# Interleaving two pairs at the changes of stretch, and taking the input sums and loads earlier

## The chip, the cores and the metric

The kernel runs on one core of one Trainium2 chip. The metric is the device time of one execution in microseconds. The engines are TensorE (PE, matmuls), VectorE (DVE), ScalarE (ACT), GpSimd (POOL) and SyncE (SP, which issues DMAs).

## The reference

Sparse attention of 2304 tokens, whose output goes through a mixture of experts (8 experts, weights from a normalised gate) and then through a second feed-forward part with an ELU. The change touches the last two.

```python
def _moe_ref(x, w_gate, w1, w2):                    # x (2304, 512), w1 (8, 512, 1024), w2 (8, 1024, 512)
    ...                                             # P (2304, 8): normalised exp(x @ w_gate)
    for e in range(E):
        h = np.maximum(x @ w1[e], 0.0)
        out += P[:, e:e + 1] * (h @ w2[e])

def _moe2_ref(x, w_in, w_out):                      # w_in (512, 2048), w_out (2048, 512)
    h = x @ w_in
    g = np.where(h > 0.0, h, alpha * (np.exp(np.minimum(h, 0.0)) - 1.0))
    return g @ w_out
```

## The kernel before

Both parts are a first product (tokens by w1 or w_in), a nonlinearity and a second product (by w2 or w_out). The hidden columns are cut into 40 pairs of 256: pairs 0 to 31 are the experts, 32 to 39 the second part. The tokens are cut into block 0 (1024 tokens), block 1 (1024) and 256 plain tokens that go with block 1. `SEGS` orders this into four **stretches**: 0 (block 0, experts), 1 (block 1 and plain tokens, experts), 2 (the same tokens, second part) and 3 (block 0, second part). The changes 0→1, 1→2 and 2→3 lie near 795, 1640 and 1865 us. Pairs are worked in groups of two: first products of both, then their second products.

Each fp32 operand is held as a high and a low part of a shorter format, and a product takes three matmuls (high·high, high·low, low·high; `products`, L934). ACT casts the high part; DVE or POOL subtract it to get the low part (`low`, L213; names `xl`, `w1l`, `w2l`, `hl`).

For a block of 1024 tokens the first product (`gemm1`) is a 2×2 block product by seven products instead of eight. Its token operands are the raw blocks B11, B21, B22 and four sums T1 to T4: t1 = b − a, t2 = b' − t1, t3 = t2 − a, t4 = a' − t2, where a, a' (tiles `rawa`) are the first half of the tokens and b, b' (`rawb`) the second. Each of the seven is a **part**: six matmuls of 128x512 into a bank. In a pair they run B11, (B21 if early), T2, T1, T3, (B21 otherwise), T4, B22. DVE adds the partial results (`add`, L995: u2 = T2's bank + a1, a copy of B11's bank by ACT, L1024; u3; c22), then `activate` makes the hidden values: ReLU on ACT (hh, L949) and its low part on DVE (hl, L951); in stretches 2 and 3 the ELU, several steps on ACT and DVE (g, hh, hl, L956 to L961). Plain tokens take `gemm1_plain` (values ph, pl).

Sum banks: `bank()` takes one of four in turn for first products, `ybank()` one of four others for second products. A bank can be taken again when its last reader is done.

The second product of a group (`whole2`, `gemm2`, L1095) runs half after half of the block; a half has four token tiles, each with a bank of its own, and 24 matmuls of the first pair come ahead of 24 of the second. `finish` has DVE add a finished bank to `acc` (L1126, L1112).

Ahead of stretches 1 and 3, whose tokens come from memory, `x_loads` issues loads of 1 MB (`rawa`, `rawb`; for stretch 1 `rawp`, the plain tokens) in the last group of the stretch before, and during that group's second product the operands are built: `build_a` (B11, B21), `x_plain`, then `x_b` with `build_b` (sums L312, casts L322, low parts L213). For stretch 2 the tokens are the stretch's own result: PE transposes `acc` (L1149), and `x1_a`, `x1_b` build from there. At the end of stretch 0 block 0's results are kept: PE transposes them, and DVE or ACT copy them (kept, L1160).

What sets the order: the program is written out by one Python thread; `gap()` is called between groups of three or six matmuls and lets each waiting generator take a step (weights, gate, builds, copies), so an engine's queue holds its instructions in the order of those steps. Each engine takes its queue strictly in order; engines wait for each other by semaphores. `need(x)` forces the build of an operand ahead of the product that reads it.

Of the kernel before, what the change touches and what calls it, by code (L numbers as in the profile page):

```python
# [123 lines left out]
def sparse_attention_moe_kernel(ctx: ExitStack, tc: tile.TileContext, a, out):  # L124
# [175 lines left out]
    def build_b(a, b, home=None, cs=(0, 1)):  # L300
# [30 lines left out]
        t3 = {c: minus(t2[c], a(c), 3, c) for c in cs}
        yield from both(T3, t3, (ve, po_))

        t4 = {c: minus(a(c + 2), t2[c], 4, c) for c in cs}
        yield from both(T4, t4, (ve, po_))
        b22 = {c: b(c + 2) for c in cs}
        yield from both(B22, b22, (ve, ve))
# [640 lines left out]
    def gemm1(sg, p, early=False):  # L978


        n = prep_state["now"] = index(sg, p)
# [70 lines left out]
        fill()  # L1052
        prod(s3, S4, B22, start=False)
        add(s3, s3, u2)
        act(s3, 0, 1)
        step()
        return hs
# [293 lines left out]
```

## Time and profile before

| what | us |
|---|---|
| runs (three) | 2035.65, 2035.70, 2038.86 |
| their median | 2035.7 |
| the profiled execution | 2036.48 |
| its span | 2034.7 |
| PE busy in it | 2000.9 (98%) |
| DVE busy | 1271.3 (62%) |
| mean granted PE clock, of full | 0.992 |

The steady stretches have no idle PE time: a group takes 40.8 us in stretch 0 and 52.0 in stretch 1. In a timeline the first column is an instruction's start in us from the start of the span, the second its duration (with x2 or x3, of all of them), and what stands in brackets is how long the engine had been idle before and which instruction's end released it. Matmuls overlap, so the distance of their starts (0.227 us at full clock) is the pace, not the duration shown.

### The profile page before, as it was taken

What the parts mean: (1) busy time and instruction counts of PE and PEld (TensorE: products, weight loads), DVE (VectorE), ACT (ScalarE), POOL (GpSimd) and SP (SyncE); (2) the same over time, 40 slices, a digit from 0 to 9 for tenths busy, and PEclk for the clock granted to TensorE, in tenths of its full rate; (3) what the DMA queues carried; (4) which work ended last, traced back from release to release, by engine and by line L of the source; (5) the groups of instructions that cost most, each with busy time, mean ns of one, the idle gap of its engine ahead of it and who ended that gap; (6) DMA issues with size and microseconds to landing.
All of it is one profiled execution on the core that took longest, in us unless ns stands there. A gap on an engine that the chain in (4) does not pass through costs nothing.

```text
span 2034.7 us, 26108 instructions
## 1 busy us (share of the span) xinstructions
PE 2000.9 (98%) x10019; PEld 1661.5 (82%) x10019; DVE 1271.3 (62%) x2061; ACT 690.3 (34%) x1419; POOL 642.2 (32%) x742
## 2 busy tenths in 40 slices
PE   8899999999999999999999999999999989999999
PEld 7677888888888887888888888888888878887887
DVE  5666757544554557466666666666664585558665
ACT  3444333322332224222222222222222354445543
POOL 3443333323233324222222222222222322224330
PEclk9899999999999999999999999999999999999999
DMA  8521111111111114122222222222221101122111
GB/s 257 152 95 60 53 55 53 59 52 43 52 62 52 42 52 139 49 91 71 82 78 83 78 83 73 80 71 88 73 68 42 42 21 42 42 83 93 42 52 52
DMA packets 82277, 145.41 MB, mean 71 GB/s; under 512 B 5689, under 2 KB 39737, under 8 KB 82153
## 3 DMA queue, kind: packets, MB, share of 16 engines
q1 hardware_dynamic: 81192, 143.55, 22.4%
q8 instruction: 78, 1.28, 0.3%
q14 instruction: 47, 0.38, 0.1%
q10 hardware_dynamic: 960, 0.21, 0.1%
HBM read 125.91 MB, written 17.83 MB: 71 GB/s over the span
## 4 chain that ended last, share of the span: by engine, by line
PE 89%; DVE 6%; ACT 3%; issue 1%; POOL 1%; DMA 0%; ACTq 0%; POOLq 0%; DVEq 0%
PE ybank L1095 46%; PE bank L934 39%; DVE xl L213 1%; ACT g L957 1%; ACT g L956 1%; PE ybank L541 1%; PE ybank L523 1%; DVE u L995 1%; PE bank L480 1%; ACT hh L961 0%; DVE rawa L312 0%; PE ybank L480 0%; DVE acc L1112 0%; DMA wg<-in_moe_w_gate 0%; DVE g L959 0%
## 5 line engine op out<-in xcount | busy, mean ns | idle before, releaser
L1095 PE MATMUL ybank<-w2h,hh 128*128 128x512 f32 x1280 | 501.5, 392 | 0.4 <-DVE acc L1112 0.2
L1095 PE MATMUL ybank<-w2h,hl 128*128 128x512 f32 x1280 | 498.2, 389 | 0.0
L1095 PE MATMUL ybank<-w2l,hh 128*128 128x512 f32 x1280 | 498.1, 389 | 0.0
L934 PE MATMUL bank<-xh,w1h 128*128 128x512 f32 x1120 | 444.4, 397 | 16.9 <-DVE u L995 5.7
L934 PE MATMUL bank<-xh,w1l 128*128 128x512 f32 x1120 | 437.9, 391 | 0.1
L934 PE MATMUL bank<-xl,w1h 128*128 128x512 f32 x1120 | 438.0, 391 | 0.0
L213 POOL TENSOR_TENSOR w1l<-w1raw,w1h 128x256 fp32r<-128x256 f32 x240 | 209.2, 892 | 425.9 <-ACT w1h L203 423.0
L1126 DVE SCALAR_TENSOR_TENSOR acc<-ybank,prob,acc 128x512 f32<-128x512 f32 x244 | 182.7, 749 | 230.3 <-PE ybank L1095 230.0
L213 POOL TENSOR_TENSOR w2l<-w2raw,w2h 128x512 fp32r<-128x512 f32 x80 | 103.6, 1295 | 569.8 <-ACT w2h L203 554.5
L1095 PEld LDWEIGHTS ybank<-w2h,hh 128*128 128x128 f32 x1280 | 240.4, 188 | 51.0 <-DVE acc L1112 1.7
L1095 PEld LDWEIGHTS ybank<-w2h,hl 128*128 128x128 f32 x1280 | 240.3, 188 | 50.3
L1095 PEld LDWEIGHTS ybank<-w2l,hh 128*128 128x128 f32 x1280 | 240.4, 188 | 48.4
L934 PEld LDWEIGHTS bank<-xh,w1h 128*128 128x128 f32 x1120 | 211.3, 189 | 67.9 <-DVE u L995 9.2
L203 ACT CAST w2h<-w2raw 128x512 fp32r<-128x512 f32 x160 | 97.0, 620 | 489.6 <-issue 396.7
L934 PEld LDWEIGHTS bank<-xh,w1l 128*128 128x128 f32 x1120 | 211.1, 188 | 45.6 <-POOL w1l L213 0.5
L934 PEld LDWEIGHTS bank<-xl,w1h 128*128 128x128 f32 x1120 | 211.6, 189 | 39.6
L995 DVE TENSOR_TENSOR u<-bank,a 128x512 f32<-128x512 f32 x160 | 110.5, 691 | 196.0 <-PE bank L934 164.6
L231 POOL TENSOR_TENSOR wsum<-w1raw 128x256 f32<-128x256 f32 x160 | 122.3, 764 | 221.6 <-DMA w1raw<-in_moe_w 159.4
L949 ACT ACTIVATE hh<-bank 128x512 fp32r<-128x512 f32 x192 | 114.2, 595 | 109.0 <-DVE bank L995 106.7
L951 DVE SCALAR_TENSOR_TENSOR hl<-bank,hh 128x512 fp32r<-128x512 f32 x192 | 131.3, 684 | 6.3
L213 DVE TENSOR_TENSOR w1l<-wsum,w1h 128x512 fp32r<-128x512 f32 (+1 forms) x164 | 119.5, 736 | 12.1 <-ACT w1h L203 11.0
L949 ACT ACTIVATE hh<-c 128x512 fp32r<-128x512 f32 x64 | 40.5, 633 | 239.1 <-DVE c L995 239.1
(194 smaller groups left out, 2541.1 us busy)
## 6 DMA issues: line engine op xcount, KB each, us to landing
w1raw<-in_moe_w SPq DMA_DIRECT2D x64, 512.0 KB, 3.4
w2raw<-in_moe_w SPq DMA_DIRECT2D x64, 512.0 KB, 3.6
q_t<-in_q SPq DMA_DIRECT2D x16, 576.0 KB, 8.0
raw<-in_moe_w_in SPq DMA_DIRECT2D x16, 512.0 KB, 4.2
w_conv<-val SPq DMA_DIRECT2D x32, 256.0 KB, 2.5
raw<-in_moe_w_out SPq DMA_DIRECT2D x16, 512.0 KB, 3.8
w1raw<-w_conv SPq DMA_DIRECT2D x16, 512.0 KB, 4.1
w2raw<-w_conv SPq DMA_DIRECT2D x16, 512.0 KB, 3.3
```

Source lines behind the costliest of these rows:

```text
L203: se.copy(hi, src)
L213: eng.tensor_tensor(out=lo, in0=src, in1=hi.bitcast(F32), op=ALU.subtract)
L231: po_.tensor_tensor(out=o, in0=x, in1=y, op=op)
L480: pe.matmul(pp[:nq, i * nk : (i + 1) * nk], t["q"][:, qc : qc + nq], t["k"][:, kc : kc + nk], start=False, stop=i == nt - 1, skip_group_ch ...
L523: pe.transpose(pt[:nk, i * nq : (i + 1) * nq], s["e"][:, i0 + i], ident[:nq, :nq])
L541: pe.matmul(pv[j * D : (j + 1) * D, c : c + nq // 2], vt[:nk, v_place(local, x if local else i + hf * len(SGROUPS[0]), j), :], es[:, j], s ...
L934: pe.matmul(dst, a_[:, wi, c, :], b_[:, xi, c, :], start=start and i == 0, stop=stop and i == 5, skip_group_check=True,)
L949: se.activation(hh, src, AF.Relu)
L951: ve.scalar_tensor_tensor(out=hl, in0=src, scalar=0.0, in1=hh.bitcast(F32), op0=ALU.max, op1=ALU.subtract)
L995: ve.tensor_tensor(out=out, in0=x, in1=y, op=ALU.add)
L1095: pe.matmul(y, x[:, cs], w[:, f], start=first and f + m == 0, stop=last and f == 1 and m == 2)
L1126: ve.scalar_tensor_tensor(out=at, in0=y, scalar=prob[:, g, e : e + 1], in1=at, op0=ALU.mult, op1=ALU.add)
```

## The change

In the first group of stretches 1, 2 and 3 the two pairs x and y run together, part by part: x B11, y B11, x B22, x B21, x T2, x T1, x T3, y B21, x T4, y T2, y T1, y T3, then plain parts (stretch 1: the second pair's, stretch 2: one), y T4, y B22. Pair x puts B22 in a bank of its own and adds it in with one more DVE add, so all three raw blocks come ahead of its sums. `build_b` gets the matching order (`raw_first`): B22, t3, T2, t4 with the subtractions ahead of the next low parts, then T1, T3, T4. The loads of stretches 1 and 3 are issued four and two groups ahead of the change, and a new generator `x_sums` makes the plain operands, t1 and t2 within those groups at a rate of 0.2 steps a gap. At 1→2 two build steps are taken in each of four gaps (`HURRY`), and the plain tokens' build starts two steps later. `OPEN_WAIT` holds the weights' preparation back by 12 gaps in an interleaved group, and `used` counts a weight's products for each pair apart.

```diff
@@ build_b @@
+        if raw_first:
+            cast = b22()
+            next(cast)
+            yield True
+            next(cast)
+            t3 = more(3)
+            yield True
+            cast = both(T2, t2, (ve, ve))
+            next(cast)
+            yield True
+            next(cast)
+            t4 = more(4)
+            yield True
+            yield from both(T1, t1, (ve, po_))
+            yield from both(T3, t3, (ve, po_))
+            yield from both(T4, t4, (ve, po_))
+            return
...
@@ gap @@
             build_step()
+            if count[0] < hurry[0]:
+                build_step()
...
+    def gemm1_two(sg, pairs, between):
+
+        landed["done"] = max(landed["done"], count[0] + OPEN_WAIT)
+        hs = [{}, {}]
+        x, y = (gemm1_parts(sg, p, h, True, p == pairs[0]) for p, h in zip(pairs, hs))
+        order = (x, y, x, x, x, x, x, y, x, y, y, y, None, y, y)
+        for part in order:
+            if part is None:
+                between()
+            else:
+                next(part)
+        return hs
...
+        if raw_first:
+            need(B22)
+            s4 = bank()
+            prod(s4, S4, B22)
+            step()
+            yield
         if early:
             c11()
+            yield
         need(T2)
         s2 = bank()
         prod(s2, S2, T2)
         u2 = tmp("u2")
         add(u2, s2, a1)
+        if raw_first:
+            add(u2, s4, u2)
+        elif early and sg:
+            tmp("skip")
         step()
+        yield
         need(T1)
         s3 = bank()
         prod(s3, S1, T1)
+        if raw_first:
+            add(s4, s3, u2)
+            act(s4, 0, 1)
         step()
+        yield
...
-    def x_plain():
+    def x_sums(plain):
...
+        if plain:
+            yield from build_plain(late["xp_raw"], *late["xp"], late_tmp)
+        late["sums"] = sums = ({}, {})
+        for c in (0, 1):
+            sums[0][c] = b[:, c]
+            ve.tensor_tensor(out=sums[0][c], in0=b[:, c], in1=a[:, c], op=ALU.subtract)
+            yield True
+        for c in (0, 1):
+            sums[1][c] = t[:, c * HALF : (c + 1) * HALF]
+            ve.tensor_tensor(out=sums[1][c], in0=b[:, c + 2], in1=sums[0][c], op=ALU.subtract)
+            yield True
...
+            if sg in (0, 2) and p == p1 - X_FROM[sg] * GROUP:
...
+                x_loads(*((x_late, True) if sg == 0 else (x_mid, False)))
+                late["x"] = x_sums(sg == 0)
+                gens.append([late["x"], X_RATE, 0.0, False])
...
-X_DELAY = 4
+X_DELAY = 8
+X_FROM, X_RATE = {0: 4, 2: 2}, 0.2
 KEEP_DELAY = 8
 LANDING = 10
+OPEN_WAIT = 12
+HURRY, PLAIN_DELAY = 4, 2
```

In the order listings the lines of the changed kernel are its own: L959 is its product, L1041 its add, L976 and L984 its steps of `activate`, L1198 its `finish`, L1221 its transposes, L1232 its keep copies.

DVE's queue in the last second product of stretch 0. Before: low parts, t1 and t2 (L312), then the accs of the second half.

```order
L213 TENSOR_TENSOR xl_70<-rawa_6579,xh_69 128x512
L213 TENSOR_TENSOR w1l0_82<-wsum_74,w1h0_81 128x512
L213 TENSOR_TENSOR xl_70<-rawa_6579,xh_69 128x512
L312 TENSOR_TENSOR rawb_6580<-rawb_6580,rawa_6579 128x512 x2
L312 TENSOR_TENSOR rawp_6581<-rawb_6580 128x512 x2
L1126 SCALAR_TENSOR_TENSOR acc_71<-ybank_6665,prob_67,acc_71 128x512
L213 TENSOR_TENSOR xl_70<-rawp_6581,xh_69 128x512 x2
L1126 SCALAR_TENSOR_TENSOR acc_71<-ybank_6666,prob_67,acc_71 128x512
```

In the changed kernel, from the same half on:

```order
L213 TENSOR_TENSOR xl_70<-rawa_5538,xh_69 128x512 x2
L1198 SCALAR_TENSOR_TENSOR acc_71<-ybank_6597,prob_67,acc_71 128x512
L1198 SCALAR_TENSOR_TENSOR acc_71<-ybank_6598,prob_67,acc_71 128x512
L213 TENSOR_TENSOR xl_70<-rawb_5539,xh_69 128x512 x2
L312 TENSOR_TENSOR rawa_5538<-rawp_5540,rawa_5538 128x512 x2
L1198 SCALAR_TENSOR_TENSOR acc_71<-ybank_6599,prob_67,acc_71 128x512
L213 TENSOR_TENSOR xl_70<-rawp_5540,xh_69 128x512 x2
L312 TENSOR_TENSOR rawa_5538<-rawa_5538,rawp_5540 128x512 x2
L1198 SCALAR_TENSOR_TENSOR acc_71<-ybank_6600,prob_67,acc_71 128x512
```

t1 and t2 are gone from here; B22's low parts, t3, T2's low parts and t4 stand between the four accs of the first half (banks 6597 to 6600), where before they stood among those of the second.

DVE's queue in the first group of stretch 1, around the first pair's u2. Before (bank 6841 is T2's, 6831 is B11's):

```order
L995 TENSOR_TENSOR u2_6849<-bank_6841,a1_6838 128x512
L213 TENSOR_TENSOR w2l0_84<-w2raw_73,w2h0_83 128x512
L995 TENSOR_TENSOR u3_6881<-bank_6841,a1_6838 128x512
L995 TENSOR_TENSOR c22_6882<-bank_6852,u3_6881 128x512
L1160 COPY kept_6888<-ybank_6873 128x512
L951 SCALAR_TENSOR_TENSOR hl_6886<-c22_6882,hh_6885 128x512
L995 TENSOR_TENSOR bank_6841<-bank_6841,a1_6838 128x512
L951 SCALAR_TENSOR_TENSOR hl_6903<-bank_6831,hh_6902 128x512
```

In the changed kernel (bank 6881 is x's T2, 6849 its B22, 6830 its B11, 6900 its T1):

```order
L1232 COPY kept_6878<-ybank_6867 128x512
L1041 TENSOR_TENSOR u2_6893<-bank_6881,a1_6837 128x512
L1041 TENSOR_TENSOR u2_6893<-bank_6849,u2_6893 128x512
L976 SCALAR_TENSOR_TENSOR hl_6876<-bank_6830,hh_6875 128x512
L1041 TENSOR_TENSOR bank_6849<-bank_6900,u2_6893 128x512
L1232 COPY kept_6917<-ybank_6904 128x512
```

PE's queue at the same place, from the end of x's T2 to its T1. Since bank 6830, x has been given 6830, y 6840, x 6849, x 6881, and then x 6900:

```order
L959 MATMUL bank_6881<-xh_69,w1h1_2250 128x512
L959 MATMUL bank_6881<-xl_70,w1h1_2250 128x512
L959 MATMUL bank_6881<-xh_69,w1l1_2251 128x512
L1221 MATMUL ybank_6885<-ident_63,acc_71 128x128 x4
L959 MATMUL bank_6881<-xh_69,w1h1_2250 128x512
L959 MATMUL bank_6881<-xl_70,w1h1_2250 128x512
L959 MATMUL bank_6881<-xh_69,w1l1_2251 128x512
L959 MATMUL bank_6900<-xh_69,w1h1_2250 128x512
L959 MATMUL bank_6900<-xl_70,w1h1_2250 128x512
```

Bank 6900 is the fifth since 6830 and so the same one of the four. hl from bank 6830 is its last read, and it has moved behind two adds u2; before, T1 took the third bank after B11's.

DVE's queue at 1→2. Before:

```order
L1126 SCALAR_TENSOR_TENSOR acc_71<-bank_13461,prob_67,acc_71 128x512
L312 TENSOR_TENSOR rawb_13476<-ybank_13482,rawb_13476 128x512
L312 TENSOR_TENSOR rawb_13476<-ybank_13492,rawb_13476 128x512
L1126 SCALAR_TENSOR_TENSOR acc_71<-bank_13462,prob_67,acc_71 128x512
L213 TENSOR_TENSOR w2l1_2254<-w2raw_73,w2h1_2253 128x512
L213 TENSOR_TENSOR xl_70<-rawb_13476,xh_69 128x512 x3
L312 TENSOR_TENSOR rawa_13376<-rawb_13476,rawa_13376 128x512 x2
L213 TENSOR_TENSOR xl_70<-rawa_13376,xh_69 128x512
L312 TENSOR_TENSOR rawa_13376<-rawa_13376,rawb_13476 128x512 x2
L995 TENSOR_TENSOR u2_13565<-bank_13554,a1_13533 128x512
L959 SCALAR_TENSOR_TENSOR g_13547<-g_13547,bank_13523 128x512
```

In the changed kernel:

```order
L312 TENSOR_TENSOR rawb_13470<-ybank_13476,rawb_13470 128x512
L312 TENSOR_TENSOR rawb_13470<-ybank_13486,rawb_13470 128x512
L213 TENSOR_TENSOR xl_70<-ybank_13476,xh_69 128x512
L213 TENSOR_TENSOR xl_70<-ybank_13486,xh_69 128x512
L312 TENSOR_TENSOR rawa_13376<-rawb_13470,rawa_13376 128x512 x2
L1198 SCALAR_TENSOR_TENSOR acc_71<-bank_13461,prob_67,acc_71 128x512
L213 TENSOR_TENSOR xl_70<-rawb_13470,xh_69 128x512 x2
L312 TENSOR_TENSOR rawa_13376<-rawa_13376,rawb_13470 128x512 x2
L1198 SCALAR_TENSOR_TENSOR acc_71<-bank_13462,prob_67,acc_71 128x512
L213 TENSOR_TENSOR w2l1_2253<-w2raw_73,w2h1_2252 128x512
L213 TENSOR_TENSOR xl_70<-rawb_13470,xh_69 128x512
L213 TENSOR_TENSOR xl_70<-rawa_13376,xh_69 128x512 x2
```

t2 (from bank and rawb) stood behind the first acc and stands ahead of it; B22's low parts (from ybank) came last and come first behind t2.

## Rows read from the trace of the kernel before

**Rows 1.** The page, busy us (share of the span) and instructions of each engine.

```profile
PE 2000.9 (98%) x10019; PEld 1661.5 (82%) x10019; DVE 1271.3 (62%) x2061; ACT 690.3 (34%) x1419; POOL 642.2 (32%) x742
```

**Rows 2.** Busy time in four stretches: us, then each engine (instructions), PEclk, DMA share, GB/s.

```profile
770.00:830.00 60.00, 57.00 (x289) 47.59 (x288) 45.14 (x66) 28.38 (x58) 30.75 (x30) 1.00 0.34 119
830.00:1630.00 800.00, 800.00 (x3875) 676.68 (x3874) 510.07 (x806) 204.37 (x426) 223.26 (x247) 1.00 0.23 72
1630.00:1675.00 45.00, 39.24 (x187) 31.18 (x186) 37.23 (x56) 27.38 (x54) 10.61 (x7) 0.92 0.07 24
1830.00:1875.00 45.00, 41.88 (x178) 33.90 (x177) 39.04 (x50) 24.45 (x48) 24.64 (x21) 0.96 0.31 106
```

**Rows 3.** PE's waits, whole span: us in total, times, longest.

```profile
PE bank L934 <- DVE u L995: 5.7, 7, 2.9
...
PE bank L934 <- ACT xh L322: 2.6, 1, 2.6
...
PE bank L934 <- ACT w1h L203: 1.4, 1, 1.4
```

**Rows 4.** Timeline of PE at 0→1: start, us, engine, line; idle time before in brackets.

```profile
799.88 0.39 PE L934 MATMUL bank<-xh,w1l 128*128 128x512 f32 x1
801.74 0.47 PE L934 MATMUL bank<-xh,w1h 128*128 128x512 f32 x1 [1.47 <-DVE kept L1160]
...
804.89 0.50 PE L934 MATMUL bank<-xh,w1h 128*128 128x512 f32 x1 [1.53 <-DVE pl L951]
```

**Rows 5.** Timeline of PE at 1→2.

```profile
1647.57 0.47 PE L934 MATMUL bank<-xh,w1h 128*128 128x512 f32 x1 [2.57 <-ACT xh L322]
...
1651.33 0.77 PE L934 MATMUL bank<-xh,w1h 128*128 128x512 f32 x1 [0.96 <-DVE u L995]
```

**Rows 6.** Busy time in one stretch at 1→2, columns as in Rows 2.

```profile
1648.00:1655.00 7.00, 6.04 (x18) 4.35 (x17) 5.21 (x9) 3.00 (x6) 2.02 (x2) 0.51 0.00 0
```

**Rows 7.** Timeline of PE at 2→3.

```profile
1866.77 0.80 PE L934 MATMUL bank<-xh,w1h 128*128 128x512 f32 x1 [2.91 <-DVE u L995]
...
1870.21 0.39 PE L934 MATMUL bank<-xh,w1l 128*128 128x512 f32 x1
```

**Rows 8.** Timeline of DVE ahead of 0→1.

```profile
774.40 1.78 DVE L343 TENSOR_TENSOR tmp<-rawp 128x512 f32<-128x512 f32 x1
...
779.90 1.52 DVE L213 TENSOR_TENSOR xpl<-rawp,xph 128x512 fp32r<-128x512 f32 x1
...
786.38 1.29 DVE L312 TENSOR_TENSOR rawb<-rawb,rawa 128x512 f32<-128x512 f32 x2
787.59 1.29 DVE L312 TENSOR_TENSOR rawp<-rawb 128x512 f32<-128x512 f32 x2
```

**Rows 9.** The DMA issues: KB of each, us from issue to landing.

```profile
rawa<-x_late SPq DMA_DIRECT2D x1, 1024.0 KB, 8.1
```

**Rows 10.** Timeline of PE in the first group of stretch 1, one row.

```profile
808.41 0.40 PE L934 MATMUL bank<-xh,w1l 128*128 128x512 f32 x1
```

**Rows 11.** Timeline of DVE behind that row.

```profile
808.85 0.69 DVE L995 TENSOR_TENSOR u<-bank,a 128x512 f32<-128x512 f32 x1 [2.48 <-PE bank L934]
809.58 0.69 DVE L995 TENSOR_TENSOR c<-bank,u 128x512 f32<-128x512 f32 x1
810.18 0.68 DVE L1160 COPY kept<-ybank 128x512 f32<-128x512 f32 x1
```

**Rows 12.** Timeline of DVE at 1→2.

```profile
1637.11 1.28 DVE L312 TENSOR_TENSOR rawb<-ybank,rawb 128x512 f32<-128x512 f32 x2
...
1639.56 3.00 DVE L213 TENSOR_TENSOR xl<-rawb,xh 128x512 fp32r<-128x512 f32 x3
...
1644.46 2.36 DVE L312 TENSOR_TENSOR rawa<-rawa,rawb 128x512 f32<-128x512 f32 x2
...
1650.51 0.68 DVE L995 TENSOR_TENSOR u<-bank,a 128x512 f32<-128x512 f32 x1
```

**Rows 13.** Timeline of GpSimd (POOL) at 1→2.

```profile
1640.16 1.85 POOL L213 TENSOR_TENSOR xl<-rawb,xh 128x512 fp32r<-128x512 f32 x1 [5.54 <-ACT xh L322]
```

More of the change, by code (lines that the diff above doesn't have):

```diff
@@ L327, in both, with b22, more @@
             yield True
+        def b22():
+            return both(B22, {c: b(c + 2) for c in cs}, (ve, ve))
+        if sums:
+            t1, t2 = sums
+        else:
+            t1 = {c: minus(b(c), a(c), 1, c) for c in cs}
+            if not raw_first:
+                yield True
+            t2 = {c: minus(b(c + 2), t1[c], 2, c) for c in cs}
+            yield True
+        def more(i):
+            return {c: minus(t2[c], a(c), 3, c) if i == 3 else minus(a(c + 2), t2[c], 4, c) for c in cs}
+        if raw_first:
[15 more added lines that the diff above has]
+            return
         yield from both(T2, t2, (ve, ve))
         yield from both(T1, t1, (ve, po_))
[L331 to L337, printed above, removed]
+        yield from both(T3, more(3), (ve, po_))
+        yield from both(T4, more(4), (ve, po_))
+        yield from b22()
     def build_plain(src, hi, lo, tmp):
@@ L790, in sparse_attention_moe_kernel @@
     gens = []
-    second = [False]
+    second, hurry = [False], [0]
     def spare_bank():
@@ L991, in prod @@
                     gap()
-            used(n, 1)
+            used(n)
         def add(out, x, y):
@@ L1051, in gemm1 @@
         step()
[L1052 to L1057, printed above, removed]
+        yield
+        if not raw_first:
+            fill()
+            prod(s3, S4, B22, start=False)
+            add(s3, s3, u2)
+            act(s3, 0, 1)
+            step()
+            yield
     def flush():
@@ L1179, in home @@
             return (t[:, c], t[:, c + 2], r[:, c], r[:, c + 2])[i - 1]
-        yield from build_b(lambda c: r[:, c], lambda c: banks[c], home)
+        yield from build_b(lambda c: r[:, c], lambda c: banks[c], home, raw_first=True)
     def x1_plain():
+        for _ in range(PLAIN_DELAY):
+            yield True
         r = late["p"].tile([P, KD, PW], F32, tag="rawp", name="rawp")
@@ L1276, in sparse_attention_moe_kernel, with between @@
             hs, hp = [], []
-            plain_last = sg == 2 and p == p0
-            for x in pairs:
-                if len(blocks) > 1 and not plain_last:
+            if sg > 0 and p == p0:
+                hp = [[] for _ in pairs] if len(blocks) > 1 else []
+                parts = [plain_parts(sg, x, h) for x, h in zip(pairs, hp)]
+                def between():
+                    if sg == 1:
+                        for _ in parts[1]:
+                            pass
+                    elif sg == 2:
+                        next(parts[0])
+                if sg == 1:
+                    for _ in parts[0]:
+                        pass
+                hs = gemm1_two(sg, pairs, between)
+                for x in parts:
+                    for _ in x:
+                        pass
+            for x in pairs[len(hs) :]:
+                if len(blocks) > 1:
                     hp.append(gemm1_plain(sg, x))
-                hs.append(gemm1(sg, x, early=sg == 2 and x == p0))
+                hs.append(gemm1(sg, x))
                 if h_prev:
```

60 lines of the change are left out of this document (35 added, 25 removed).

## The prediction

> **What bounds the kernel now.** I read the page's busy times first, then busy time by stretch, then TensorE's (PE's) list of waits, and last the timelines of the three places at which those waits lie. PE is busy 98% of the span [rows 1], so only two things can move the time: the number of matmuls, which this change leaves as it is, and the places where PE stands or runs slowly. PE is busy for every one of the 800 us from 830 to 1630; around the three changes of stretch it idles 3.0, 5.8 and 3.1 us [rows 2]. The list of waits says who ends these: VectorE's (DVE's) adds and ScalarE's casts [rows 3].
>
> A part of the first product is six matmuls; at full clock each starts 0.227 us behind the last, so a part takes 1.36. Counting by the starts of successive matmuls, PE loses against that pace 4.2 us around change 0→1 (770 to 830), 12.6 around 1→2 (1630 to 1830) and 5.9 around 2→3 (1830 to 1905): some 23 us, all that this change can win.
>
> At 0→1 there are two stops. The start at 799.88 is followed by 801.74, that is 1.86 − 0.23 = 1.63 lost, of which the row names 1.47; the other, named with 1.53, cost 1.69 by the same count [rows 4]. The rest, 0.9, is transposes, which stay. The clock is full there. At 1→2 the timeline has stops of 2.57 and 0.96 [rows 5]; from 1648 to 1655 the granted clock is 0.51 [rows 6], the lower of the two levels, 1.2 GHz, and 14 matmuls start 0.43 apart: 14 × 0.2 = 2.8 us. At 2→3 one stop of 2.91 (3.07 by starts) is followed by half clock: the eight matmuls from 1866.77 to 1870.21 take 3.44 where full pace wants 1.81, so 1.6 [rows 7].
>
> **The change, 0→1.** The two pairs' parts interleave, so an input is needed one or more parts later than before, and the plain inputs, t1 and t2 leave this stretch. Off DVE's queue here go the plain difference (1.78), the plain low part (1.52), t1 and t2 (1.29 for two, each) [rows 8]: 5.9 us. Both stops waited for work queued behind those, so I count both gone: −3.3. The moved operations land in groups of the steady stretch, and the moved loads (8.1 us to landing [rows 9]) have a second product, some 20 us, of lead: nothing. Were that cover gone, a wait for all four sums would cost at most their 2.6 us. The later preparation of weights, the two build steps in a gap and the delayed plain inputs I also set at nothing, since a whole group lies between a weight and its use; without that cover it is a wait like the one for w1h, 1.4 [rows 3].
>
> New is a wait that before does not have. PE's pool of sum banks has four. x's B11, y's B11, x's B22 and x's T2 hold four, so x's T1 is the fifth and takes x's first bank again; the order shows hl, its last reader, behind both adds u2 (one add more than before). So T1 waits for T2's end, two dependent adds, and hl. The steady stretch prices it: the last matmul of a T3 starts at 808.41 [rows 10] and u at 808.85 (+0.44), the dependent c at 809.58 (+0.73), the next independent operation at 810.18 (+0.60), and that takes 0.68 [rows 11]; I allow 0.1 until PE starts. 0.44 + 0.73 + 0.60 + 0.68 + 0.1 = 2.55 from the start of T2's last matmul, where 0.23 is the pace: **+2.3 at each of the three changes**, not below 0, and not above 3.7 (two more operations ahead of hl).
>
> The second new cost lies in the last second product of the stretch. There the order puts B22's low parts, t3, T2's low parts and t4, eight operations with both inputs in SBUF, and an acc ahead of the fourth acc of the first half; the fourth bank of the second half waits for that acc. The first half's banks are done 1.36 apart, the second near 780.6, the fourth near 783.1, and the second half's fourth bank is wanted three parts later, at 787.2. DVE goes on from the second acc's end at 781.3: eight operations at 0.61, DVE's pace beside an idle GpSimd [rows 8], and two accs of 0.65 make 787.5; at 0.9 an operation it is 789.8. That slower pace is near what 1→2 shows: three low parts in 3.00, two sums in 2.36, while GpSimd ran a low part in 1.85 [rows 12, 13]. GpSimd works part of the time here, so between 0.4 and 2.7 I take the middle, **+1.6**. Sum at 0→1: −3.3 + 2.3 + 1.6 = **+0.6**, between −1.0 and +2.
>
> The Trainium skill says here (SBUF — State Buffer, "Who interferes with whom") that a DVE instruction with two SBUF inputs contends with a GpSimd instruction that reads SBUF, and that the second is blocked for the first one's whole length. The 3.00 for three agrees with it. By that rule, if the operations overlapped all along, the sum at 0→1 would be near +2; without it, −0.6. It speaks against packing these operations ahead of acc.
>
> **1→2.** Here the inputs are the stretch's own results, so only the order can help. DVE is the bound: from t2 at 1637.11 to the second u at 1650.51 it hardly idles [rows 12], and PE has done five parts of the first pair when it starts again at 1651.33 [rows 5]. The change keeps the work and moves t2 ahead of the acc before it, so that the chain starts at 1635.2. Its length: 1650.5 − 1637.1 = 13.4, plus that acc (0.7), less u and g (1.2), which now follow: 12.9. It ends near 1648.1; two adds u2 and the ELU's g (2.0) and PE's start put x's T1 at 1650.3. Again five parts are done: **−1.0**. Uncontended, three low parts take 1.8 and two sums 1.2 instead of 3.00 and 2.36, 2.5 us less: T1 starts at 1647.8, −3.5, and the eight half-clock matmuls behind 1651.33 (8 × 0.2 = 1.6) may go as well: −5.1. If T2's low parts and t4 meet GpSimd's low parts more than now, +2 (two more operations at double length, and the clock lower for four matmuls more). The small waits of the second pair, 4.3 us up to 1675, I leave as they are.
>
> **2→3.** Removed: 3.07 and the half clock behind it, 1.6. Added: T1's bank, +2.3; acc, wanted at 1852.9 by the count used at 0→1 and given between 1852.0 and 1854.4, so 0 to 1.5, of which I take 1.0; and in the second pair waits of y's T3 for u2 and of y's T4 for u3, between DVE's ELU steps, some 2.0 where before lost 0.8: +1.2. Sum: −4.7 + 4.5 = **−0.2**, between −1.6 and, with the clock lower again, +3.4.
>
> **Sum.** +0.6 − 1.0 − 0.2 = −0.6. The profiled execution took 2036.5 us, 1.8 above its span and 0.8 above the median of the runs; against its own time the sum gives 2035.9, against the median 2035.7 − 0.6 = **2035.1**. A difference within 0.2% (4.1 us) can hardly be told from none in this kernel: the forecast is no change.
>
> **Rivals.** *Faster:* GpSimd's few operations do not overlap DVE's two-input ones in the new order, which then run at 0.61. acc costs 0.4 and 0, T1 at 1→2 comes at 1647.8, the clock holds. 0→1: −3.3 + 2.3 + 0.4 = −0.6; 1→2: −5.1; 2→3: −4.7 + 2.3 + 1.2 = −1.2. Sum −6.9: 2028.8. For it: in 784 to 789 DVE ran eight such operations at 0.61. Against: the 3.00 and 2.36.
>
> *Slower:* GpSimd's reads hold DVE in the last second products, at 0.9 us or more an operation. PE's stops there grow to 2.7 and the clock falls, as it fell behind stops of 2.6 and 2.9 [rows 5, 7], at 0→1 too, where 1.5 did not bring it down [rows 4]. 0→1: −3.3 + 2.3 + 2.7 + 1.6 = +3.3; 1→2: 0, for the contended chain; 2→3: −4.7 + 2.3 + 1.5 + 1.2 + 1.6 = +1.9. Sum +5.2: 2040.9. It decides from a pace of 0.9 on. For it are the 3.00 and 2.36; against it, that GpSimd idles much of the time. It is the result that the Trainium skill's rule in "SBUF — State Buffer", named above, would give.
>
> *It does not do what it says:* interleaving and early sums stand in the order, but if the total of DVE's work and not its order sets the stops, all three stay: 2035.7.
>
> **How the numbers follow.** Forecast 0.50, faster rival 0.32, slower 0.14, nothing moved 0.04: faster 0.32, within 0.2% 0.54, slower 0.14. The range goes past the faster rival's time by 0.8, to 2028.0, since its 1→2 term is the least certain, and ends short of the slower rival's, at 2040.0; about a tenth is left out on each side.
>
> **What would show it.** Gone from PE's list: the waits for kept and pl at 0→1 and the one of 2.9 for u at 2→3. In their place three waits of a first T1 matmul for hl or g, 2.1 to 2.4 each; one wait of a second-product matmul for acc in the last group of stretches 0 and 2; at 1→2, x's T1 starting between 1647.8 and 1651. I am wrong if the T1 wait is missing or under 1 us, if the granted clock stays full behind all three changes (faster), or if acc stands in the list with 2.5 or more at 0→1 (slower). PE should stay without idle time from 830 to 1630; if not, the moved loads or sums cost what I set at nothing.

## The result and the profile after

The changed kernel took 2054.8 us (median of four runs, 2051.7 to 2060.3) where the kernel before took 2037.2 (2035.65 to 2038.86): a ratio of 1.0089, 95% interval 1.0065 to 1.0113. It is slower by 0.9%; the forecast of no change was wrong, and the time lies above the whole range. Single runs of one kernel differ by up to 10 us. Up to 8 of them lie in the attention ahead of 270 us, which the change leaves alone: in the profiled executions of before, after, again, both and mix the granted clock averaged 0.96 from 0 to 270 us, in mix_ve 0.94, in the other six 0.92, and the same wait for acc that the changed kernel ends at 786.85 ends at 794.95 in bank_free. So below the three changes of stretch are compared by place, and times by the ratio of runs on the same chip; the two need not agree to a few us.

The profiled execution took 2051.7 us, 15.2 more than that of before. Busy time by stretch, as in [rows 2]:

```profile
770.00:830.00 60.00, 54.61 (x263) 44.89 (x262) 41.73 (x55) 24.65 (x48) 22.59 (x21) 0.94 0.23 76
830.00:1630.00 800.00, 800.00 (x3874) 676.75 (x3873) 511.00 (x808) 206.07 (x432) 223.82 (x250) 1.00 0.22 72
1630.00:1675.00 45.00, 37.98 (x173) 30.64 (x172) 35.33 (x49) 22.09 (x42) 14.19 (x11) 0.92 0.07 24
1850.00:1900.00 50.00, 42.34 (x162) 32.88 (x161) 36.04 (x46) 20.12 (x36) 20.27 (x17) 0.90 0.25 87
```

PE is still busy for all of the 800 us in the middle. Around 0→1 it idles 5.4 us instead of 3.0, and the granted clock is 0.94 instead of 1.00; around 2→3 it idles 7.7 and the clock is 0.90. Who ends that idle time stands in PE's list of waits (in total, times, longest):

```profile
PE bank L959 <- DVE u L1041: 5.9, 6, 2.4
PE bank L959 <- DVE g L984: 5.7, 2, 3.5
...
PE ybank L1167 <- DVE acc L1184: 3.5, 2, 3.3
PE ybank L1167 <- DVE acc L1198: 3.2, 2, 2.5
...
PE bank L959 <- DVE hl L976: 2.2, 1, 2.2
```

The waits for kept and pl [rows 4] and the one of 2.9 for u [rows 7] are gone. In their place stand the ones that the prediction named: acc (3.2 and 3.5), and hl and g, on which the first T1 matmul waits. In PE's timeline:

```profile
786.85 0.50 PE L1167 MATMUL ybank<-w2h,hh 128*128 128x512 f32 x1 [0.72 <-DVE acc L1198]
...
791.01 0.55 PE L1167 MATMUL ybank<-w2h,hh 128*128 128x512 f32 x1 [2.50 <-DVE acc L1198]
791.36 0.63 PE L1167 MATMUL ybank<-w2l,hh 128*128 128x512 f32 x1
...
814.82 0.51 PE L959 MATMUL bank<-xh,w1h 128*128 128x512 f32 x1 [2.18 <-DVE hl L976]
...
1655.95 0.79 PE L959 MATMUL bank<-xh,w1h 128*128 128x512 f32 x1 [3.50 <-DVE g L984]
...
1863.78 0.79 PE L1167 MATMUL ybank<-w2h,hh 128*128 128x512 f32 x1 [3.30 <-DVE acc L1184]
...
1882.73 0.50 PE L959 MATMUL bank<-xh,w1h 128*128 128x512 f32 x1 [2.17 <-DVE g L984]
```

786.85, 791.01 and 1863.78 are second-product matmuls (L1167) that wait for a bank whose acc DVE has not done; 814.82, 1655.95 and 1882.73 are the first T1 matmuls of the three stretches. 791.36 shows what a row at the lower clock looks like: 0.63 instead of 0.39, and the next start is 0.43 away.

What PE lost against 0.227 us a matmul of 128x512, counted by the starts of successive matmuls as in the prediction, for the profiled execution of every kernel told of here:

| kernel | 0→1 (740 to 840) | 1→2 (1600 to 1832) | 2→3 (1832 to 1915) | sum | ratio of runs to before (95%) |
|---|---|---|---|---|---|
| before | 4.2 | 13.1 | 6.0 | 23.3 | |
| after | 10.1 | 14.0 | 14.2 | 38.3 | 1.0089 (1.0065 to 1.0113) |
| again | 10.0 | 14.0 | 12.1 | 36.1 | 1.0074 (1.0048 to 1.0100) |
| bank_free | 5.7 | 10.0 | 9.7 | 25.4 | 1.0043 (1.0029 to 1.0056) |
| fine | 5.2 | 13.0 | 6.9 | 25.1 | 1.0018 (1.0003 to 1.0033) |
| quiet | 3.5 | 11.8 | 6.4 | 21.7 | 1.0034 (1.0019 to 1.0048) |
| early | 1.9 | 11.7 | 2.8 | 16.4 | 0.9980 (0.9966 to 0.9994) |
| both | 0.6 | 8.7 | 4.8 | 14.1 | 0.9966 (0.9952 to 0.9980) |
| ve_lows | 0.6 | 9.1 | 4.0 | 13.7 | 0.9959 (0.9945 to 0.9973) |
| plain_late | 0.6 | 12.9 | 4.0 | 17.5 | 0.9989 (0.9976 to 1.0002) |
| mix | 0.6 | 8.6 | 3.6 | 12.8 | 0.9951 (0.9933 to 0.9968) |
| mix_ve | 0.6 | 9.0 | 3.6 | 13.2 | 0.9954 (0.9937 to 0.9972) |

38.3 − 23.3 = 15.0, nearly all of the 15.2 us, lie at the three changes. Counting the small matmuls (transposes, plain tokens) in another way moves an entry by up to 0.4. The kernels from again on are the experiments.

### The profile page after: what moved, and what is told of

Same layout as the page of the kernel before. It is cut to its first block, busy times and chain, and to the rows that moved or that the text cites. A ratio compares the mean times of both kernels' runs of the same rounds, so it can differ in the third digit from the quotient of the medians.

```text
span 2049.9 us, 26103 instructions
## 1 busy us (share of the span) xinstructions
PE 2006.9 (98%) x10019; PEld 1665.4 (81%) x10019; DVE 1279.3 (62%) x2064; ACT 692.1 (34%) x1419; POOL 643.6 (31%) x742
## 3 DMA queue, kind: packets, MB, share of 16 engines
q8 instruction: 78, 1.28, 0.3%
## 4 chain that ended last, share of the span: by engine, by line
PE 90%; DVE 6%; ACT 3%; issue 1%; POOL 1%; DMA 0%; ACTq 0%; POOLq 0%; DVEq 0%
PE ybank L1167 46%; PE bank L959 40%; DVE xl L213 1%; ACT g L982 1%; DVE u L1041 1%; ACT g L981 1%; PE ybank L564 1%; PE ybank L546 1%; DVE rawa L312 1%; PE bank L503 1%; DVE g L984 0%; ACT hh L986 0%; PE ybank L503 0%; DMA wg<-in_moe_w_gate 0%; DVE e_t L512 0%
## 5 line engine op out<-in xcount | busy, mean ns | idle before, releaser
L1167 PE MATMUL ybank<-w2h,hh 128*128 128x512 f32 x1280 | 503.7, 394 | 6.9 <-DVE acc L1184 3.5
L1167 PE MATMUL ybank<-w2l,hh 128*128 128x512 f32 x1280 | 500.0, 391 | 0.0
L1167 PE MATMUL ybank<-w2h,hl 128*128 128x512 f32 x1280 | 499.9, 391 | 0.0
L959 PE MATMUL bank<-xh,w1h 128*128 128x512 f32 x1120 | 444.9, 397 | 17.9 <-DVE u L1041 5.9
L959 PE MATMUL bank<-xl,w1h 128*128 128x512 f32 x1120 | 438.8, 392 | 0.0
L959 PE MATMUL bank<-xh,w1l 128*128 128x512 f32 x1120 | 438.4, 391 | 0.1
L1198 DVE SCALAR_TENSOR_TENSOR acc<-ybank,prob,acc 128x512 f32<-128x512 f32 x244 | 182.8, 749 | 224.8 <-PE ybank L1167 224.1
L1167 PEld LDWEIGHTS ybank<-w2h,hh 128*128 128x128 f32 x1280 | 241.3, 189 | 59.4 <-DVE acc L1184 5.8
L1167 PEld LDWEIGHTS ybank<-w2h,hl 128*128 128x128 f32 x1280 | 241.4, 189 | 50.7
L1167 PEld LDWEIGHTS ybank<-w2l,hh 128*128 128x128 f32 x1280 | 241.4, 189 | 48.7
L959 PEld LDWEIGHTS bank<-xh,w1h 128*128 128x128 f32 x1120 | 211.6, 189 | 68.2 <-DVE u L1041 10.5
L959 PEld LDWEIGHTS bank<-xh,w1l 128*128 128x128 f32 x1120 | 211.6, 189 | 45.7 <-POOL w1l L213 0.5
L959 PEld LDWEIGHTS bank<-xl,w1h 128*128 128x128 f32 x1120 | 211.8, 189 | 39.7
L1041 DVE TENSOR_TENSOR u<-bank,a 128x512 f32<-128x512 f32 x160 | 110.6, 691 | 199.6 <-PE bank L959 169.4
L976 DVE SCALAR_TENSOR_TENSOR hl<-bank,hh 128x512 fp32r<-128x512 f32 x192 | 131.3, 684 | 6.2
```

Of the source, the lines that this page charges most:

```text
L959: pe.matmul(dst, a_[:, wi, c, :], b_[:, xi, c, :], start=start and i == 0, stop=stop and i == 5, skip_group_check=True,)
L976: ve.scalar_tensor_tensor(out=hl, in0=src, scalar=0.0, in1=hh.bitcast(F32), op0=ALU.max, op1=ALU.subtract)
L1041: ve.tensor_tensor(out=out, in0=x, in1=y, op=ALU.add)
L1167: pe.matmul(y, x[:, cs], w[:, f], start=first and f + m == 0, stop=last and f == 1 and m == 2)
L1198: ve.scalar_tensor_tensor(out=at, in0=y, scalar=prob[:, g, e : e + 1], in1=at, op0=ALU.mult, op1=ALU.add)
```

## The experiments

Theory A: the loss follows from the order of DVE's queue. Two-input operations that GpSimd slows stand ahead of acc, and the last read of x's first bank stands behind two adds; PE stops at both places, and behind a long stop its clock is lower for some matmuls. Rivals: B, the clock falls by itself in these groups; C, DVE's total of work is the bound, so that a wait removed comes back elsewhere; D, DVE is slow there for another reason than GpSimd.

### again: the changed kernel once more

> The changed kernel once more, unaltered, as the base of this set. Theory A (queue order): the stops stand where they stood, within 0.3 us of their length (acc 2.5 in the last second product of stretch 0 and 3.3 in that of stretch 2; a first T1 matmul behind hl or g 2.2, 3.5, 2.2), since each follows from the order in the queues; runs differ only in how long the clock stays at its lower level behind them. Theory B (the clock falls by itself in these groups, whatever the stops): runs differ in where the clock falls. Median 2051 to 2058 by either.

Median 2051.2 us (2049.3 to 2059.7). The stops of its profiled execution are those of the first, to 0.05 us: acc 2.5 and 3.3, T1 2.2, 3.5 and 2.2; only one wait for u at 2→3 was longer (2.4 for 1.4). The half clock was not the same: at 2→3 it cost 2.0 us where the first execution had 5.1. So the stops are fixed by the order, and what the clock adds behind them is not. A's expectation held, but for that u; it is the longer (2.4, in fine and quiet too) where the matmuls behind the T1 stop ahead of it ran at full clock, so part of what half clock costs there takes the place of a wait.

### bank_free: x's first bank is read ahead of the adds

```diff
         u2 = tmp("u2")
+        if raw_first:
+            advance(acts)
         add(u2, s2, a1)
         if raw_first:
             add(u2, s4, u2)
```

> The changed kernel with one edit: the hidden values of x's first bank take their next step ahead of the two adds u2, so that its last reader is done during T2's product. Theory A: the waits of the first T1 matmul go below 0.5 at 0->1 and 2->3 (2.2 each), with the half clock behind them (1.8 and 1.5), and at 1->2, where the inputs come late anyway, 3.5 becomes 2.5 to 3: together -7 to -9, a median near 2047. Theory B: the waits go, 5 us, and the half clock stays: -5. Rival C (DVE's total work in the opening group is the bound): the wait moves to x's T3 or y's T-parts and less than 3 us are won.

Median 2047.3 us, ratio 1.0043, where 2047 was expected. PE's waits:

```profile
PE bank L959 <- DVE u L1041: 4.3, 6, 1.3
...
PE ybank L1169 <- DVE acc L1186: 3.5, 2, 3.3
PE ybank L1169 <- DVE acc L1200: 3.2, 2, 2.5
...
PE bank L959 <- DVE g L984: 2.9, 2, 2.2
```

hl is gone from the list, g is 2.9 instead of 5.7, and acc is as it was (3.5 and 3.2). What is left of g is 2.2 at 1→2 and 0.7 at 2→3. The loss falls by 4.4 at 0→1, by 4.0 at 1→2 and by 4.5 (2.4 against again) at 2→3. At 0→1 that is the stop (2.35) and 2.0 of half clock, which goes from 2.9 to 0.9 us and is now behind the acc stop alone. At 1→2 it is 1.3 of the wait for g, 1.4 of the one for u behind it (2.6 to 1.1) and some half clock; at 2→3, against again, 1.45 of the T1 stop and 1.2 of the wait for u, and the half clock is as before (2.2 and 2.0). So C falls. One profile doesn't decide on B; the later ones do: both, ve_lows, plain_late, mix and mix_ve have no stop at 0→1, and none of the five has half clock there.

### fine: one DVE operation a step of the build

```diff
             for c in cs:
                 low(hi[:, x, c], lo[:, x, c], t[c], engs[c])
                 built.add((x, c))
+                if sums and c == 0:
+                    yield True
             yield True
...
-            next(cast)
-            t3 = more(3)
+            if sums:
+                yield from cast
+            else:
+                next(cast)
+            t3 = yield from more(3)
             yield True
```

`more` likewise yields between its two subtractions, and t4 follows the same pattern; the build at 1→2 stays as it was.

> The changed kernel with one edit: ahead of stretches 1 and 3 the build takes one DVE operation a step instead of four, so that the fourth acc of the first half stands behind three of the eight two-input operations instead of all. Theory A: the waits for acc (0.7 and 2.5 at 0->1, 3.3 at 2->3) go below 0.7 in all and the half clock behind them too (1.6 and 2.8); T1's waits stay at 2.2: -8 to -11, a median near 2044. Rival C: the low parts that now come later are missed by the opening parts (a wait for xl of 2 us or more), and less than 3 us are won. Theory B: 6 us of waits go, half clock stays: -6.

Median 2043.8 us, ratio 1.0018, where 2044 was expected. PE's waits:

```profile
PE bank L974 <- DVE g L999: 5.7, 2, 3.5
...
PE bank L974 <- DVE hl L991: 2.2, 1, 2.2
...
PE ybank L1236 <- DVE acc L1213: 1.1, 1, 1.1
...
PE ybank L1182 <- DVE acc L1199: 0.2, 1, 0.2
```

The second product (L1182) waits 0.2 for acc in all, where it waited 6.7; the 1.1 left is that of transposes at 1→2, which stands in the changed kernel's profile too and not in that of before. T1's waits stand as they did. The loss at 0→1 falls by 4.9, at 2→3 by 7.3 (5.2 against again). No stop for a late low part came in exchange: C falls here too. The same amount of DVE work in another order takes 7.5 us off the median of again.

### quiet: GpSimd silent in the last second products

```diff
     def low(hi, lo, src, eng):
+        if still[0] and eng is po_:
+            return
         eng.tensor_tensor(out=lo, in0=src, in1=hi.bitcast(F32), op=ALU.subtract)
...
-            po_.tensor_tensor(out=o, in0=x, in1=y, op=op)
+            if not still[0]:
+                po_.tensor_tensor(out=o, in0=x, in1=y, op=op)
```

> The changed kernel without GpSimd's operations in the last second products of stretches 0 and 2 (its low parts of inputs and weights and its weight sums are left out there); DVE's and ScalarE's queues are as they were. Theory A, with GpSimd's reads as the cause of DVE's pace: B22's and T2's low parts, t3 and t4 run at 0.60 to 0.65 each instead of 0.9 to 1.45, the fourth acc comes 2 to 4 us earlier, the waits for acc fall to at most 0.5 at both places and the half clock behind them goes: -7 to -10. Rival D (DVE is slow there for another reason, ScalarE or the loads): the pace stays at 0.9 or more and the waits for acc stay within 0.5 of 2.5 and 3.3.

Median 2044.8 us, 6.4 under again, a little less than expected. By place the profile lost 14.4 less at the three changes (21.7 against 36.1); it ran at 0.92 and not 0.96 in the attention, so the times show less than that. DVE's queue between two of the accs of the first half, first in the changed kernel:

```profile
780.74 0.75 DVE L1198 SCALAR_TENSOR_TENSOR acc<-ybank,prob,acc 128x512 f32<-128x512 f32 x1 [0.61 <-PE ybank L1167]
781.40 2.98 DVE L213 TENSOR_TENSOR xl<-rawb,xh 128x512 fp32r<-128x512 f32 x2
784.31 1.82 DVE L312 TENSOR_TENSOR rawa<-rawp,rawa 128x512 f32<-128x512 f32 x2
786.06 0.74 DVE L1198 SCALAR_TENSOR_TENSOR acc<-ybank,prob,acc 128x512 f32<-128x512 f32 x1
786.72 2.38 DVE L213 TENSOR_TENSOR xl<-rawp,xh 128x512 fp32r<-128x512 f32 x2
789.01 1.28 DVE L312 TENSOR_TENSOR rawa<-rawa,rawp 128x512 f32<-128x512 f32 x2
790.22 0.74 DVE L1198 SCALAR_TENSOR_TENSOR acc<-ybank,prob,acc 128x512 f32<-128x512 f32 x1
```

and with GpSimd silent:

```profile
788.60 0.75 DVE L1203 SCALAR_TENSOR_TENSOR acc<-ybank,prob,acc 128x512 f32<-128x512 f32 x1 [0.61 <-PE ybank L1172]
789.27 1.28 DVE L217 TENSOR_TENSOR xl<-rawb,xh 128x512 fp32r<-128x512 f32 x2
790.47 1.28 DVE L317 TENSOR_TENSOR rawa<-rawp,rawa 128x512 f32<-128x512 f32 x2
791.67 0.74 DVE L1203 SCALAR_TENSOR_TENSOR acc<-ybank,prob,acc 128x512 f32<-128x512 f32 x1
792.34 1.28 DVE L217 TENSOR_TENSOR xl<-rawp,xh 128x512 fp32r<-128x512 f32 x2
793.54 1.28 DVE L317 TENSOR_TENSOR rawa<-rawa,rawp 128x512 f32<-128x512 f32 x2
794.74 0.74 DVE L1203 SCALAR_TENSOR_TENSOR acc<-ybank,prob,acc 128x512 f32<-128x512 f32 x1
```

From start to start (successive operations overlap a little, so their durations add up to more) the eight two-input operations take 4.66 + 3.50 = 8.2 us, 1.02 each, beside GpSimd, and 2 × 2.40 = 4.8, 0.60 each, without it; the accs, which read a bank and acc, take 0.74 or 0.75 in both. From the second acc's start to the fourth's it is 9.5 and 6.1 us, and PE waits 0.2 for acc instead of 6.7. D falls. The Trainium skill's rule that the prediction cited (SBUF — State Buffer, "Who interferes with whom") agrees: operations of DVE with two SBUF inputs lose time against GpSimd's reads, and the ones that read a bank do not: the acc at 780.74 takes 0.75 though GpSimd works from 780.70 on.

### early: only the loads and sums, on the kernel before

```diff
+                x_loads(*((x_late, True) if sg == 0 else (x_mid, False)))
+                late["x"] = x_sums(sg == 0)
+                gens.append([late["x"], X_RATE, 0.0, False])
...
-        t1 = {c: minus(b(c), a(c), 1, c) for c in cs}
-        yield True
-        t2 = {c: minus(b(c + 2), t1[c], 2, c) for c in cs}
-        yield True
+        if sums:
+            t1, t2 = sums
+        else:
...
```

> The kernel before with one part of the change alone: the earlier loads, the plain operands and t1, t2 in the steady groups; its own order of parts and of the build stays. By theory A and the prediction's count the stops for kept and pl at 0->1 (1.6 and 1.7) go, and the stop for u at 2->3 (3.1, DVE's queue) shrinks by the 2.5 to 3 us of sums taken out, with its half clock: -5 to -7, ratio 0.9965 to 0.998. Rival: the stops at 0->1 and 2->3 are set by what stays in the queue (low parts, t3, t4), and less than 2 us are won.

Median 2036.9 us, ratio 0.9980 (0.9966 to 0.9994); the profile's losses say −6.9, the runs −4. At 0→1 two stops of 0.6 and 0.5 are left of 1.6 and 1.7, at 2→3 one of 1.5 of 3.1, with no half clock behind it. So this part of the change did what it says, and it alone makes the kernel faster, by a little (the interval ends at 0.9994); the interleaving as written lost more than this won.

### both: bank_free and fine together

> The changed kernel with the edits of bank_free and fine together. Theory A: their gains add up, since they remove different stops: no acc wait over 0.3 and no T1 wait over 0.9 at 0->1 and 2->3; what is left of the losses at the three changes is near 2, 10 and 5 us, 17 to 20 with the small ones behind, where the kernel before lost 25: 5 to 8 us under before, ratio 0.996 to 0.998. Rival C (the total of DVE's work is the bound): a new stop over 1.5 us at 0->1 or 2->3, and a ratio of 1.000 or more.

Median 2035.0 us, ratio 0.9966 (0.9952 to 0.9980): under the kernel before, as expected. PE's waits, of those that lie at the changes:

```profile
PE bank L974 <- DVE u L1056: 4.3, 6, 1.3
...
PE bank L974 <- DVE g L999: 2.9, 2, 2.2
...
PE ybank L1238 <- DVE acc L1215: 1.1, 1, 1.1
...
PE ybank L1184 <- DVE acc L1201: 0.2, 1, 0.2
```

At 0→1 nothing is left but the transposes' 0.6. The two edits add up: at 0→1 they win 4.4 and 4.9 alone and 9.5 together. At 1→2 the loss is 8.7, under the 13.1 of before and the 11.7 of early; in bank_free, ve_lows, mix and mix_ve it is between 8.6 and 10.0. So the interleaving is of use there once the bank is free in time, though only part of the gain is stops (some 6.6 us of them in before, 5.8 here); the rest is half clock, which varies. Over early, both's gain of 2.3 at the three changes is the profile's alone: the intervals of their runs overlap. What `HURRY` and `OPEN_WAIT` add by themselves was not run.

### ve_lows: the low parts all on DVE

```diff
-            yield from both(T1, t1, (ve, po_))
-            yield from both(T3, t3, (ve, po_))
-            yield from both(T4, t4, (ve, po_))
+            yield from both(T1, t1, (ve, ve))
+            yield from both(T3, t3, (ve, ve))
+            yield from both(T4, t4, (ve, ve))
```

> As both, and T1's, T3's and T4's second low parts go to DVE instead of GpSimd (three operations at each change). If a GpSimd operation that overlaps blocks DVE for its length (1.1 to 1.2 beyond the 0.61 that DVE needs for the operation itself), the chain at 1->2 from t2 to g gets 1 to 2 us shorter although DVE does more, and T1 starts that much earlier: 1 to 3 us under both, with less half clock. Rival (GpSimd takes work off DVE as meant): the chain gets three times 0.61 longer, +1 to +2 over both.

DVE at 1→2 from t1 to g, in both:

```profile
1632.44 0.69 DVE L312 TENSOR_TENSOR rawb<-ybank,rawa 128x512 f32<-128x512 f32 x1 [0.45 <-PE ybank L1238]
...
1639.45 3.12 DVE L213 TENSOR_TENSOR xl<-rawb,xh 128x512 fp32r<-128x512 f32 x2
...
1644.96 1.78 DVE L213 TENSOR_TENSOR xl<-rawb,xh 128x512 fp32r<-128x512 f32 x1
...
1647.87 0.68 DVE L999 SCALAR_TENSOR_TENSOR g<-g,bank 128x512 f32<-128x512 f32 x1
```

and in ve_lows:

```profile
1638.09 0.69 DVE L312 TENSOR_TENSOR rawb<-ybank,rawa 128x512 f32<-128x512 f32 x1 [0.45 <-PE ybank L1238]
...
1645.09 1.28 DVE L213 TENSOR_TENSOR xl<-rawb,xh 128x512 fp32r<-128x512 f32 x2
...
1649.96 2.49 DVE L213 TENSOR_TENSOR xl<-rawa,xh 128x512 fp32r<-128x512 f32 x4
1652.36 0.68 DVE L999 SCALAR_TENSOR_TENSOR g<-g,bank 128x512 f32<-128x512 f32 x1
```

With three more operations in it the chain takes 14.3 us (1638.09 to 1652.36) instead of 15.4: the two low parts of T2 take 1.28 instead of 3.12, and four of the last take 2.49. A GpSimd low part that overlaps costs DVE about 1.0 us, against 0.6 for doing it itself. The total doesn't show it: ratio 0.9959, its interval overlapping that of both, since at 1→2 half clock took back what the stops gave (9.1 us lost against 8.7). Nor do the medians, 2031.0 and 2035.0: the shortest runs are 2026.9 and 2026.7, the longest 2036.3 and 2035.6.

### plain_late: the plain tokens' transposes six gaps later

> As both, with the transposes of the plain tokens at 1->2 six gaps later (PLAIN_DELAY 8 for 2). They wait for the plain tokens' last acc, which stands behind low parts in DVE's queue (1.1 us in PE's list), and PE's products stand behind them. Theory A: that stop goes, but x's T1 waits for DVE's chain anyway, so the wait for g grows by the same and the time is that of both within 1 us. Rival (the stop is paid in full): -1.1 to -1.5.

Neither: the ratio is 0.9989 and the loss at 1→2 rises from 8.7 to 12.9. The stop at the transposes moved: PE's list has a wait of 1.2 for an acc, now of a first-product matmul, and new ones where the plain products need what comes out of the transposes, 1.9 in two for ScalarE's high parts, 1.1 for the low part on GpSimd and 0.3 for the one on DVE, with half clock behind them.

### mix and mix_ve: stretch 3 opened as before

```diff
-            if sg > 0 and p == p0:
+            if sg in (1, 2) and p == p0:
...
-                start_build((sg + 1, "b"), x_b())
+                start_build((sg + 1, "b"), x_b(sg == 0))
```

The build's new order (`raw_first`) is thus used ahead of stretch 1 and not ahead of stretch 3.

> As both, but stretch 3 opens as in the kernel before (pairs one after the other, the build's old order), with the early loads and sums kept: the part of the change that showed no use at 2->3, since early lost 2.8 us there and both 4.8. Theory A: 2->3 as in early (one stop for u near 1.5), 0->1 and 1->2 as in both: 1 to 2 us under both, 6 to 8 under before, ratio 0.9955 to 0.997. Rival: with one operation a step the old order comes too late at 2->3 and the stop for u is 2.5 or more: no better than both.

> As mix, with T1's, T3's and T4's second low parts on DVE as in ve_lows. If overlap with GpSimd is what costs at 1->2, x's T1 there starts 1 us or more earlier than in mix and the total is 0.5 to 2 us lower; if GpSimd takes work off DVE, the same or 1 to 2 us higher. At 2->3 two more operations of 0.61 stand ahead of u: the stop there grows by at most 1.2 unless the overlap costs more than that.

mix: median 2029.2 us, ratio 0.9951 (0.9933 to 0.9968), the fastest here, faster than the kernel before and the changed one. The loss at 2→3 is 3.6 against 4.8 in both, with one stop of 1.0; the interval overlaps that of both, so the last step is shown by the profile and not by the runs. mix_ve (0.9954) can't be told from mix; its chain at 1→2 is again 14.3 against 15.4.

## Why the prediction was wrong, step by step

**What bounds the kernel** held: nearly all of the time came from the three changes, and the steady stretch kept PE busy. One small thing was set at nothing and was not: the moved sums cost 0.5 us near 682, where they stand between DVE's adds of a first product.

**The stops removed** held: −3.3 at 0→1 and −4.7 at 2→3 are gone from the profile, and early wins most of them without the rest.

**T1's bank** held: 2.55 − 0.23 = 2.3 was forecast, and PE lost 2.35 at 0→1 and 2.33 at 2→3; bank_free removes it at 0→1 and leaves 0.9 of it at 2→3. At 1→2 the first T1 matmul waits 3.5, for DVE's chain first. The working from [rows 10, 11] was exact because the same chain (product, add, dependent add, next operation) stood in the trace of before.

**acc** is the step that failed first. Its mechanism was right, its size was not: 1.6 at 0→1 and 1.0 at 2→3 were forecast, 0.88 + 2.67 = 3.55 and 3.46 were lost, both above the upper end of 2.7 and 1.5. The prediction took the middle between a pace of 0.61 and one of 0.9; the pace was 1.02, with which its own sum (781.3 + 8.2 + 1.3 = 790.8, wanted at 787.2) gives the 3.6 that was lost. [rows 12] had it: three in 3.00 is 1.0 and two in 2.36 is 1.18, which the text rounded down to 0.9 as its end. The reason given for the middle, that GpSimd works only part of the time, came without a row for this place. In it GpSimd has low parts of the same build and of the weights in its queue, as its timeline in the changed kernel shows, and they meet DVE's:

```profile
780.70 1.45 POOL L213 TENSOR_TENSOR w1l<-w1raw,w1h 128x256 fp32r<-128x256 f32 x2
782.10 1.74 POOL L213 TENSOR_TENSOR xl<-rawb,xh 128x512 fp32r<-128x512 f32 x1
783.80 1.18 POOL L213 TENSOR_TENSOR w1l<-w1raw,w1h 128x256 fp32r<-128x256 f32 x1
786.86 1.68 POOL L213 TENSOR_TENSOR xl<-rawa,xh 128x512 fp32r<-128x512 f32 x1 [1.88 <-ACT xh L317]
```

DVE ran at 0.61 in 784 to 789 of before, which the prediction counted for the faster rival; there GpSimd is idle from 783.3 to 788.8, and the change moves such operations into the few us in which it is not. The prediction also looked only at the fourth bank, where the third waits too (0.88).

**Half clock** is the larger miss. The sum held no half clock behind any new stop, and gives no reason: the acc stops, at their measured 2.7 and 3.5, were as long as those of before that had it (2.6 and 2.9), and the T1 stops of 2.3 nearly so. Matmuls that started 0.08 to 0.2 us late add up to 3.8 us at 0→1, of which 0.9 are the transposes of before, so half clock is 2.9 there; at 2→3 it is 5.1. The prediction had put this into the slower rival at 1.6 a place, and there only once a place; its range at 2→3 reaches +3.4, about what half clock behind both stops gives by its own terms (0.3 + 3.2), but the sum does not. With it and with acc at its measured price:

- 0→1: −3.3 + 2.35 + 3.55 + 2.9 = +5.5, measured 10.1 − 4.2 = +5.9 (forecast +0.6).
- 2→3: −4.7 + 2.33 + 3.46 + 5.1, and y's waits for u, 1.56 + 0.95 − 0.8 = 1.7 (forecast 1.2): +7.9, measured +8.2 (forecast −0.2).
- 1→2: forecast −1.0, measured +0.9. DVE's chain from t1 to x's T1 takes 17.5 us (1638.46 to 1655.95), as in before (1633.75 to 1651.33, 17.6), where the forecast of 1650.3 makes it 16.6. Moving t2 ahead won nothing, since more operations met GpSimd: t3 (2.35 for two), T2's low parts (3.11 for two) and the one of T1's (1.79) took 4.0 us over the uncontended pace, where before lost 3.0 (3.00, 2.36 and 1.45). The rest is new stops, at the transposes for acc (1.1) and behind T1 for u (2.4) and ph (0.9). All stops there add up to some 8.6 us, against 6.6 in before; half clock did not add to it, it cost about 1 us less.

The two chains start here, first in before and then, with T2's low parts, in the changed kernel:

```profile
1633.75 0.69 DVE L312 TENSOR_TENSOR rawb<-ybank,rawa 128x512 f32<-128x512 f32 x1 [1.81 <-PE ybank L1149]
...
1638.46 0.69 DVE L312 TENSOR_TENSOR rawb<-ybank,rawa 128x512 f32<-128x512 f32 x1 [0.45 <-PE ybank L1221]
...
1645.48 3.11 DVE L213 TENSOR_TENSOR xl<-rawb,xh 128x512 fp32r<-128x512 f32 x2
```

**The rivals.** The slower one was the right mechanism at the wrong price and with too small a chance: 2040.9 at 0.14, measured 2054.8. Its own condition, a pace of 0.9 or more, was met by the rows that stood beside it, and its sign, acc with 2.5 at 0→1, came true (2.50). The faster one needed a pace of 0.61, which only quiet reached, with GpSimd silent.

## What to carry to other kernels

Where a two-input DVE operation stands ahead of something that PE waits for, price it at what such operations cost beside GpSimd in the same place (here 0.9 to 1.2 and not 0.6), and don't carry over a pace from a place in which GpSimd is idle. Before an operand is moved up, look for what it is moved past: here eight operations, in two steps of four, went ahead of one acc, and one operation a step took the waits for acc from 6.7 us to 0.2. When a bank is taken again, its last reader belongs ahead of the adds that don't need it. And a new stop is never charged at its own length alone: the clock behind it is a term of its own, and in these profiles it ranged from nothing to nearly the length of the stop.

## What the runs showed of the hardware

The same stop is not always followed by half clock. Busy time around the T1 stop at 2→3 (2.33 us in both executions; the third number from the end is the granted clock), in the changed kernel's first profile:

```profile
1880.00:1887.00 7.00, 4.83 (x15) 3.51 (x14) 2.68 (x4) 2.36 (x5) 0.00 (x0) 0.76 0.00 0
```

and in again, the same program:

```profile
1878.00:1885.00 7.00, 4.83 (x22) 3.68 (x21) 3.68 (x6) 2.90 (x6) 0.00 (x0) 1.00 0.00 0
```

0.76 in the one and 1.00 in the other, as in fine and quiet. In the profiles here, stops of 2.3 to 2.7 us had between none and eleven matmuls at half clock behind them, those of 3.5 to 3.7 between none and fourteen. The Trainium skill (TensorE: Matmul & The Clock Gate, "Part 1: The HAM clock gate (the 'warmup' mystery)") says that the number of slow matmuls at the start of one kernel varies from run to run; these profiles show the same behind stops in its middle. What decides it, these runs don't show; it makes a profile's loss at a change uncertain by some 2 to 3 us (14.2 and 12.1 at 2→3 in two executions of one program), and it is part of why ve_lows and both can't be told apart.

And work given to GpSimd to relieve DVE can cost DVE more than doing it: in ve_lows and mix_ve a low part that DVE does itself takes 0.6, where one that GpSimd does beside it adds about 1.0 to DVE's chain.
